# A GeGLU feed-forward kernel on one core: `w_down` staged two rows a step, S3 in one subtraction

## The chip, the cores and the metric

The kernel runs on one core of one Trainium2 chip. The metric is the device time of one execution in microseconds (us); the time of a kernel is the median of its runs. A core has a matmul engine (TensorE, PE in the profile, with its weight loads as PEld), a vector engine (VectorE, DVE), a scalar engine (ScalarE, ACT), a general engine (GpSimd, POOL), and SyncE (SP), which here only issues DMAs. Each engine works through its own queue in order: an instruction that waits holds up all behind it. PSUM, into which TensorE writes, has 8 banks of 128 x 512 fp32.

## The reference

```python
B, S, D, F = 1, 2048, 1024, 3584          # all bf16
# x: (B, S, D); w_gate, w_up: (D, F); w_down: (F, D)
def _gelu(x):
    return jax.nn.gelu(x, approximate=True)

def reference(x, w_gate, w_up, w_down):
    return (_gelu(x @ w_gate) * (x @ w_up)) @ w_down
```

Three matrix products, with Gelu and an elementwise product between them.

## The kernel before, in words

**Seven products for eight.** Each matrix product is made by Winograd's form of Strassen's scheme: both operands are cut into 2 x 2 blocks, sums of blocks are formed (S1 to S4 and a copy of block 22 on the weight side, T1 to T4 and a copy of B22 on the other), and seven block products M1 to M7 take the place of eight. The sums are made in fp32r, so most matmuls read fp32r operands.

**Halves, chunks, pairs.** The 2,048 rows of x are worked in two halves `h` of 1,024 rows, each as two blocks of 512 (`xT[0]`, `xT[1]`, transposed). F has 28 tiles of 128 columns; four tiles make a chunk of `w_gate` and `w_up` (`chunks`, 1 MB each). Two tiles make a *pair*; 14 pairs make a half. The result, `hT`, holds 28 tiles x 1,024 rows in bf16. The free part of `hT` is borrowed before it is written: chunks 0 and 4 lie in its tiles 20 to 27, held M1 results in others.

**The first half runs as** `first_units` (plain products of eight tiles for block 0; the first half of each sum, which is M1, is kept by `hold` and later fetched back into a bank), then `quads` over `MID` (pairs 4, 5), then `quads` over `LEADS` (eight pairs, made of tiles 0 to 7 and 12 to 19, whose M1 is a held one), then the loop over `lead` with two pairs each: lead 10 and lead 12 (pairs 10, 11 and 12, 13), which begin with M1 and M2 of both pairs in plain bf16. Then `down_group` twice: the product with `w_down`.

**A pair in `quads`** issues, for gate (j = 0) and up (j = 1): M5 and M6 (in `LEADS` the order is M5 of gate, M6, M6, M5 of up; elsewhere M6 first), each of 4 matmuls into a bank of 512 columns; ScalarE copies M5 to `m5` and M6 on to the R banks; VectorE adds M5 (`add_m5`, L497); M7 (reads S3); V = R + M5 (L497 again); M3 onto the Q banks (reads S4, needs the addition), M4 onto the R banks. ScalarE applies Gelu to the gate bank, VectorE multiplies with the up bank into `hT` (L305), which frees the bank. Meanwhile the sums of the *next* pair are made: S1, S2, S4 by GpSimd (L449), the copy of A22 by ScalarE (L462), S3 by GpSimd, or by VectorE (L447) where `s3_dve` is set (MID and LEADS).

**The staging.** T2 and T4 of `w_down` are needed four times (two halves, two groups). They are computed once in the first half and kept in DRAM (`t_dram`); the down phase loads them. `stage_load` fetches row block i and row block 14 + i of `w_down` into one `wd_sb` buffer (three of them); `stage_step` is one of three subtractions for row i: t = b12 - b11 (k = 0), t = b22 - t (k = 1, stored as T2), t' = b21 - t (k = 2, stored as T4). 14 rows make 42 steps of 512 columns (L685, stores at L687), with `t` in one of four `o_sb` buffers. The steps are placed by hand, in lists `thens[n][name]` that `quads` runs after a product (`done(n, name)`; "start" is ahead of the pair's first product): each runs on VectorE behind the pair's own work there.

**x of the second half.** Block 1 goes straight into `xT[1]` (DMA transposes at L201). Block 0 has no room yet: `stage_x` transposes it into tiles 24 to 27 of `hT` (L704), and `store_x` writes it to `x_dram` (L709), before pairs 12 and 13 write those tiles.

**Order.** `sp`, `act`, `dve`, `pool` and `pe` chain all instructions of an engine in the order in which the program writes them. Waits for data and for buffers are added by the framework, by regions of memory. All weight rows, t stores, x transposes and x stores go through SP's queue; the chunks of `w_gate` and `w_up` in this stretch go through ScalarE's.

Of the kernel before, what the change touches and what calls it, by code (L numbers as in the profile page):

```python
# [34 lines left out]
def kernel(  # L35
# [50 lines left out]
    o_pool = ctx.enter_context(tc.tile_pool(name="o", bufs=4))  # L86
# [11 lines left out]
    s_late = []  # L98

# [71 lines left out]
    chunks = {}  # L171

    def new_chunk(key):
        if key in ((0, 0), (0, 4)):
            mem, c0 = hT0[:, HF : HF + KD, :].rearrange("p a b -> p (a b)"), 0
        else:
            mem, c0 = w_mem, 2 * CH * (key[1] % 2 if key != (0, 3) else 0)
        chunks[key] = tuple(
            mem[:, c0 + j * CH : c0 + (j + 1) * CH].rearrange(
                "p (a b) -> p a b", b=FG  # L180
            )
            for j in range(2)
        )
# [108 lines left out]
    def gelu(ps, last=False):  # L292

        if last:
            g_sb = o_pool.tile([P, TB], F32, name="o_sb")[:]
        else:
            e0 = 4 * CH + (g_ctr[0] % 4) * 2 * TB
            g_ctr[0] += 1
            g_sb = w_mem[:, e0 : e0 + 2 * TB].bitcast(F32)
        act(nc.scalar.activation(out=g_sb, in_=ps[:], func=ACT.Gelu_apprx_tanh))  # L300
        return g_sb
# [163 lines left out]


    def quads(hT, h, members, nxt, thens, m5_first, plain=True, s3_dve=False):
# [6 lines left out]
        def fetch(n):  # L474
            for j in range(2):
                act(nc.scalar.copy(out=bank2(run[n][4][j]), in_=p_hold(n, j)))
# [32 lines left out]
        if not plain:  # L509
            fetch(0)  # L510
# [9 lines left out]
        for n, (pair, after, then, _, Q_) in enumerate(run):  # L520
# [3 lines left out]
            def prep(j, name, after=after):  # L524
                if after is not None:
                    on_dve = s3_dve and name == "s3"
                    s_sum(after[0], after[1], j, name, on_dve, False)
# [85 lines left out]
    def load_b21(n, q):  # L613
        i0, i1 = q * BPT, min((q + 1) * BPT, NS)
        if i1 < NS:
            w = wd_pool.tile([P, WDT, D], BF16, name="wd_sb")
            w = w[:].rearrange("p a d -> p (a d)")
        else:
            w = o_pool.tile([P, (i1 - i0) * DN], BF16, name="o_sb")[:]
        w = w.rearrange("p (b n) -> p b n", n=DN)  # L620
        src = wdv[:, NS + i0 : NS + i1, 0:DN]
        sp(nc.sync.dma_start(out=w[:, 0 : i1 - i0, :], in_=src))
        b21_tiles[(n, q)] = w
# [41 lines left out]
    NSTEP = 3 * NS  # L665

    def stage_load(i):
        w = wd_pool.tile([P, WDT, D], BF16, name="wd_sb")
        for j in range(2):
            k = j * NS + i  # L670
            sp(nc.sync.dma_start(out=w[:, j : j + 1, :], in_=wdv[:, k : k + 1, :]))
        staged[i] = [w]

    def stage_step(n):
        i, k = n // 3, n % 3
        w = staged[i][0]
        if k != 1:
            staged[i].append(o_pool.tile([P, DN], F32R, name="o_sb")[:])
        t = staged[i][-1]
        in0, in1 = (  # L680
            lambda: (w[:, 0, DN:D], w[:, 0, 0:DN]),
            lambda: (w[:, 1, DN:D], t.bitcast(F32)),
            lambda: (w[:, 1, 0:DN], staged[i][1].bitcast(F32)),
        )[k]()
        dve(nc.vector.tensor_tensor(out=t, in0=in0, in1=in1, op=ALU.subtract))  # L685
        if k > 0:
            sp(nc.sync.dma_start(out=t_dram[:, i, k - 1, :], in_=t.bitcast(F32)))  # L687

# [47 lines left out]
    def down_group(hT, h, grp, then):  # L736
# [65 lines left out]
        def evacuate(bset, l, d, halves=False):  # L802

            outs = []
            for u in range(2):
                if halves and u == 1:
                    r0 = h * SH + t0 + (2 * l + u) * P
                    for bank, c in ((bset[u], 0), (VB[u], DH)):
                        dst = o_pool.tile([P, DN], BF16, name="o_sb")[:, 0:DH]
# [8 lines left out]
                dst = o_pool.tile([P, DN], BF16, name="o_sb")[:]  # L818
# [118 lines left out]
    for h in range(NH):  # L937
# [16 lines left out]
        nstep, loads = len(steps), list(range(3, NS))  # L954
# [9 lines left out]

        def run_loads():
            while loads and 3 * (loads[0] - 2) <= nstep - len(steps):
                stage_load(loads.pop(0))
# [7 lines left out]
        if h == 0:  # L975
            for i in range(3):
                stage_load(i)

            def load_half(c, f0):
                if f0 == 0:  # L980
                    new_chunk((0, c))
                for j in range(2):
# [9 lines left out]
                    "m4": [lambda: new_x(1), lambda: run_steps(1)],  # L992
                },
                {
                    "start": [lambda: run_steps(1)],
                    "m5": [lambda: load_half(3, FA)],
                    "m3": [lambda: run_steps(1), run_loads],
                    "m4": [lambda: run_steps(1)],
# [4 lines left out]
            for n in range(NL):  # L1003
                thens[n]["start"] = [lambda: run_steps(1), run_loads]
                thens[n]["m3"] = [lambda n=n: run_steps(1 + n % 2), run_loads]
# [6 lines left out]
            thens[7]["start"].append(lambda: load_half(5, FA))  # L1012
# [6 lines left out]
        for lead in range(begin, NPAIR, PPG):  # L1019
# [7 lines left out]
            if h == 0:  # L1027
                add(0, "m1", lambda: run_steps(4), run_loads)
                if lead < NPAIR - PPG:
                    add(0, "start", lambda: run_steps(3))  # L1030
                add(1, "start", lambda: run_steps(1))
                for n in range(PPG):
                    add(n, "start", run_loads, run_x)
                    add(n, "m4", store_x, run_loads)
                    add(n, "m3", lambda: run_steps(1), run_loads)
                    add(n, "m4", run_late)
# [122 lines left out]
```

## Time and profile before

| | |
|---|---|
| runs | 544.23, 545.2, 545.32 us; median 545.2 us |
| profiled execution | 543.92 us, span 542.1 us |
| PE, DVE, ACT, POOL busy | 534.5, 385.3, 272.8, 246.3 us |
| steps (L685) | 42, 48.7 us together (28 of 1086 ns, 14 of 1304 ns) |
| S3 on DVE (L447, into s_mem) | 20, some 1.04 us each |
| DMA, `w_down` to `wd_sb`, staging | 28 of 256 KB |
| DMA, `o_sb` to `t_dram` | 28 of 256 KB |

By stage, from the span's start (PE's busy time beside the length): MID ends and LEADS begin near 59 us; LEADS last to 137.7 (DVE busy 76.4 of 78.8 us); lead 10 to 160.5, lead 12 to 187; the down phase of the first half to 275; the second half's pairs to 451 and its down phase to the end.

How to read it: times are of one profiled execution. L481 is the line that issues the matmuls of `quads`, L758 those of the down phase. "idle before, releaser" names what ended an engine's wait. Matmuls are pipelined, so a busy PE is not a PE at its peak: a row of 4 lasts 4 x 0.228 us, though each is shown with about 0.39.

### The profile page before, as it was taken

What the parts mean: (1) busy time and instruction counts of PE and PEld (TensorE: products, weight loads), DVE (VectorE), ACT (ScalarE), POOL (GpSimd) and SP (SyncE); (2) the same over time, 40 slices, a digit from 0 to 9 for tenths busy, and PEclk for the clock granted to TensorE, in tenths of its full rate; (3) what the DMA queues carried; (4) which work ended last, traced back from release to release, by engine and by line L of the source; (5) the groups of instructions that cost most, each with busy time, mean ns of one, the idle gap of its engine ahead of it and who ended that gap; (6) DMA issues with size and microseconds to landing.
All of it is one profiled execution on the core that took longest, in us unless ns stands there. A gap on an engine that the chain in (4) does not pass through costs nothing.

```text
span 542.1 us, 7109 instructions
## 1 busy us (share of the span) xinstructions
PE 534.5 (99%) x2380; PEld 381.1 (70%) x2380; DVE 385.3 (71%) x498; ACT 272.8 (50%) x471; POOL 246.3 (45%) x202
## 2 busy tenths in 40 slices
PE   9999999999999999999999999999999999999997
PEld 4448787777676776767668686767768686866866
DVE  0497999999887999789565253434444659979861
ACT  4465666556554418216565555546555552462270
POOL 0088988988397200000045494949587670000000
PEclk9999999999999999999999999999999999999999
DMA  8963647495767696878960404223140329677846
GB/s 238 273 226 101 211 127 212 117 327 172 243 166 269 203 384 218 301 242 290 321 234 0 157 13 144 73 83 122 34 155 5 151 68 333 230 246 249 290 143 209
DMA packets 98292, 102.70 MB, mean 189 GB/s; under 512 B 18768, under 2 KB 73168, under 8 KB 98256
## 3 DMA queue, kind: packets, MB, share of 16 engines
q1 hardware_dynamic: 71792, 82.53, 47.1%
q10 hardware_dynamic: 26464, 19.73, 12.1%
q8 instruction: 19, 0.31, 0.2%
q14 instruction: 17, 0.14, 0.1%
HBM read 85.98 MB, written 12.58 MB: 182 GB/s over the span
## 4 chain that ended last, share of the span: by engine, by line
PE 90%; DVE 4%; DMA 3%; issue 2%; ACT 1%; SPq 0%; DVEq 0%; ACTq 0%
PE bank L481 53%; PE bank L758 31%; PE bank L342 5%; DVE o_sb L685 2%; DMA t_mem<-t_dram 1%; DMA x_dram<-hT 1%; DVE hT L305 1%; PE bank L232 1%; DVE bank L497 0%; SPq L709 0%; PE bank L324 0%; ACT w_mem L300 0%; ACT bank L542 0%; ACT bank L507 0%; DVE xT L332 0%
## 5 line engine op out<-in xcount | busy, mean ns | idle before, releaser
L481 PE MATMUL bank<-t_mem,s_mem 128*128 128x512 f32 x1096 | 254.7, 392 | 2.9 <-ACT bank L542 0.9
L481 PEld LDWEIGHTS bank<-t_mem,s_mem 128*128 128x128 f32 x1096 | 205.0, 188 | 50.0 <-POOL s_mem L449 2.7
L449 POOL TENSOR_TENSOR s_mem<-w_mem 128x512 fp32r<-128x512 bf16 x80 | 97.1, 1232 | 190.3 <-DVE t_mem L287 99.3
L305 DVE TENSOR_TENSOR hT<-w_mem,bank 128x512 bf16<-128x512 f32 x106 | 71.2, 683 | 69.8 <-PE bank L481 39.5
L497 DVE TENSOR_TENSOR bank<-bank,m 128x512 f32<-128x512 f32 x112 | 72.7, 692 | 42.7 <-ACT m L537 41.0
L758 PE MATMUL bank<-t_mem,s_mem 128*128 128x512 f32 x416 | 98.4, 394 | 0.4 <-DMA t_mem<-t_dram 0.4
L300 ACT ACTIVATE w_mem<-bank 128x512 f32<-128x512 f32 x106 | 62.6, 596 | 60.7 <-DVE bank L497 39.0
L758 PEld LDWEIGHTS bank<-t_mem,s_mem 128*128 128x128 f32 x416 | 78.0, 188 | 17.8 <-DVE t_mem L660 0.8
L481 PE MATMUL bank<-xT,w_mem 128*128 128x512 bf16 x320 | 71.0, 379 | 0.4 <-DVE hT L305 0.4
L660 DVE TENSOR_TENSOR t_mem<-w_mem 128x1024 fp32r<-128x1024 bf16 x56 | 65.7, 1218 | 0.4 <-PE bank L481 0.4
L449 POOL TENSOR_TENSOR s_mem<-w_mem,s_mem 128x512 fp32r<-128x512 bf16 x46 | 61.2, 1352 | 3.4 <-PE bank L481 3.4
L481 PEld LDWEIGHTS <-w_mem 128*128 128x128 bf16 x320 | 30.6, 98 | 38.5 <-issue 3.0
L449 POOL TENSOR_TENSOR s_mem<-s_mem,w_mem 128x512 fp32r<-128x512 f32 x46 | 57.3, 1265 | 0.2
L542 ACT COPY bank<-bank 128x512 f32<-128x512 f32 x56 | 31.9, 571 | 29.6 <-PE bank L481 20.4
L462 ACT CAST s_mem<-w_mem 128x512 fp32r<-128x512 bf16 x48 | 29.5, 616 | 24.4 <-PE bank L481 23.2
L537 ACT COPY m<-bank 128x512 f32<-128x512 f32 x56 | 32.7, 588 | 17.5 <-PE bank L481 15.8
L758 PEld LDWEIGHTS <-hT 128*128 128x128 bf16 x224 | 21.2, 98 | 26.7 <-issue 2.1
L823 ACT CAST o_sb<-bank 128x512 bf16<-128x512 f32 x27 | 14.8, 586 | 33.8 <-PE bank L758 31.2
L685 DVE TENSOR_TENSOR o_sb<-wd_sb,o_sb 128x512 fp32r<-128x512 bf16 x28 | 30.4, 1086 | 0.3
L758 PE MATMUL bank<-t_mem,s_late 128*128 128x512 f32 (+1 forms) x132 | 30.3, 382 | 0.0
L507 ACT COPY bank<-bank 128x512 f32<-128x512 f32 x40 | 22.8, 570 | 12.6 <-PE bank L481 12.6
L730 DVE TENSOR_TENSOR s_mem<-hT 128x512 fp32r<-128x512 bf16 x36 | 23.5, 686 | 7.0 <-PE bank L758 7.0
(61 smaller groups left out, 398.6 us busy)
## 6 DMA issues: line engine op xcount, KB each, us to landing
t_mem<-t_dram SPq DMA_DIRECT2D x56, 512.0 KB, 5.5
wd_sb<-in_w_down_dram SPq DMA_DIRECT2D x28, 256.0 KB, 3.5
t_dram<-o_sb SPq DMA_DIRECT2D x28, 256.0 KB, 2.4
w_mem<-in_w_gate_dram ACTq DMA_DIRECT2D x6, 1024.0 KB, 5.3
w_mem<-in_w_up_dram ACTq DMA_DIRECT2D x6, 1024.0 KB, 8.1
wd_sb<-in_w_down_dram SPq DMA_DIRECT2D x12, 512.0 KB, 7.6
w_mem<-in_w_gate_dram SPq DMA_DIRECT2D x8, 512.0 KB, 5.5
w_mem<-in_w_up_dram SPq DMA_DIRECT2D x8, 512.0 KB, 7.2
```

What stands on the lines that cost most here:

```text
L300: act(nc.scalar.activation(out=g_sb, in_=ps[:], func=ACT.Gelu_apprx_tanh))
L305: nc.vector.tensor_tensor(out=hT[:, fc, tb * TB : (tb + 1) * TB], in0=g_sb, in1=ps[:], op=ALU.mult,)
L342: nc.tensor.matmul(banks[held[u][j]][:], lhsT=w_sb[:, kd, f0 : f0 + P], rhs=xT[0][:, kd, :], start=kd == 0, stop=kd in (KH - 1, KD - 1), s ...
L449: pool(nc.gpsimd.tensor_tensor(out=t, in0=in0, in1=in1, op=op))
L462: act(nc.scalar.copy(out=t, in_=a(1, 1)))
L481: nc.tensor.matmul(banks[bank][:], lhsT=lhs[:, c, :], rhs=rhs[:, c, :], start=start and c == 0, stop=c == KH - 1, skip_group_check=True,)
L497: nc.vector.tensor_tensor(out=banks[dst][:], in0=banks[src][:], in1=m5[:], op=ALU.add)
L537: act(nc.scalar.copy(out=m5[j][:], in_=banks[V_[j]][:]))
L542: act(nc.scalar.copy(out=banks[R_[j]][:], in_=banks[Q_[j]][:]))
L660: dve(nc.vector.tensor_tensor(out=t, in0=in0, in1=in1, op=ALU.subtract))
L685: dve(nc.vector.tensor_tensor(out=t, in0=in0, in1=in1, op=ALU.subtract))
L758: nc.tensor.matmul(banks[bank][:, c0:c1], lhsT=lhs(i, u), rhs=rhs(i)[:, c0:c1], start=start and i == 0, stop=stop and i == NS - 1, skip_gr ...
```

## The change

One `o_sb` buffer pool of four is replaced by one strip of memory (`o_mem`) of four slots, handed out in turn by `new_o`; a slot is 128 x 512 fp32. A step now works on two rows at once: 1,024 columns, two slots, so that the strip holds two such tiles, one for k = 0 and 1, the other for k = 2. `stage_load` brings two row blocks in one DMA of 512 KB; a load m is issued when `first_step(m)` steps have been issued. There are 21 steps, one for each pair of MID and LEADS (at "m3") and eleven in leads 10 and 12: two at "m1" and two at "start" of each, one after M3 of pairs 10, 11 and 12. `s3_both` makes both S3 of a pair in one subtraction, after M7 of up. The M1 of the first LEADS pair is fetched after M7 of the second MID pair, not at the head of LEADS. `stage_x` of block 0 and `store_x` move from leads 10 and 12 into the last LEADS pair (start, m3, m4).

```diff
--- before.py
+++ after.py
@@ -83,7 +83,6 @@
     hT_pool = ctx.enter_context(tc.tile_pool(name="hT", bufs=1))
     wd_pool = ctx.enter_context(tc.tile_pool(name="wd", bufs=3))
     m_pool = ctx.enter_context(tc.tile_pool(name="m5", bufs=1))
-    o_pool = ctx.enter_context(tc.tile_pool(name="o", bufs=4))
     dram_pool = ctx.enter_context(
         tc.tile_pool(name="dram", bufs=1, space=bass.MemoryType.DRAM)
     )
@@ -96,6 +95,17 @@
 
     s_mem = shared_pool.tile([P, 2 * 5 * KH * P], F32R, name="s_mem")
     s_late = []
+
+    NO = 4
+    o_mem = shared_pool.tile([P, NO * 2 * DN], BF16, name="o_sb")
+    o_ctr = [0]
+
+    def new_o(dtype, n=1):
+        o0 = o_ctr[0] % NO * DN
+        assert o0 + n * DN <= NO * DN
+        o_ctr[0] += n
+        o = o_mem[:, 2 * o0 : 2 * (o0 + n * DN)]
+        return o if dtype == BF16 else o.bitcast(dtype)
 
     CH = KD * FG
     w_mem = shared_pool.tile([P, 4 * CH + (NS - 4) * DN], BF16, name="w_mem")
@@ -168,13 +178,16 @@
         return banks[bank][:].rearrange("p (b c) -> p b c", b=2)
 
     xs0 = w_mem[:, 4 * CH : 4 * CH + TSB * D].rearrange("p (a b) -> p a b", b=D)
-    chunks = {}
+    chunks, both = {}, {}
 
     def new_chunk(key):
         if key in ((0, 0), (0, 4)):
             mem, c0 = hT0[:, HF : HF + KD, :].rearrange("p a b -> p (a b)"), 0
         else:
             mem, c0 = w_mem, 2 * CH * (key[1] % 2 if key != (0, 3) else 0)
+        both[key] = mem[:, c0 : c0 + 2 * CH].rearrange(
+            "p (j a b) -> p j a b", j=2, b=FG
+        )
         chunks[key] = tuple(
             mem[:, c0 + j * CH : c0 + (j + 1) * CH].rearrange(
                 "p (a b) -> p a b", b=FG
@@ -292,7 +305,7 @@
     def gelu(ps, last=False):
 
         if last:
-            g_sb = o_pool.tile([P, TB], F32, name="o_sb")[:]
+            g_sb = new_o(F32)
         else:
             e0 = 4 * CH + (g_ctr[0] % 4) * 2 * TB
             g_ctr[0] += 1
@@ -463,6 +476,24 @@
 
     S_NAMES = ("s1", "s2", "s3", "s4", "a22")
 
+    def s3_both(h, pair):
+        s0 = 2 * S_NAMES.index("s3") * KH * P
+        t = s_mem[:, s0 : s0 + 2 * KH * P]
+        t = t.rearrange("p (j a b) -> p j a b", j=2, b=P)
+        for j in range(2):
+            ssum[(h, pair, j, "s3")] = t[:, j]
+        ins = []
+        for tile_ in tiles_of(h, pair):
+            f0 = tile_ % FPG * P
+            ins.append(both[(h, tile_ // FPG)][:, :, half(0), f0 : f0 + P])
+        dve(
+            nc.vector.tensor_tensor(out=t, in0=ins[0], in1=ins[1], op=ALU.subtract)
+        )
+
+
+    def fetch_to(bset, n):
+        for j in range(2):
+            act(nc.scalar.copy(out=bank2(bset[j]), in_=p_hold(n, j)))
 
     def quads(hT, h, members, nxt, thens, m5_first, plain=True, s3_dve=False):
 
@@ -472,8 +503,7 @@
             run.append((pair, after, thens[n], (PB, RB)[n % 2], (QB, VB)[n % 2]))
 
         def fetch(n):
-            for j in range(2):
-                act(nc.scalar.copy(out=bank2(run[n][4][j]), in_=p_hold(n, j)))
+            fetch_to(run[n][4], n)
 
         def mm(bank, lhs, rhs, start):
             for c in range(KH):
@@ -506,8 +536,6 @@
                 mm(first_[j], block((h, "p", pair), j, 0, 0), b11, True)
                 act(nc.scalar.copy(out=banks[q_[j]][:], in_=banks[first_[j]][:]))
         done(0, "m1")
-        if not plain:
-            fetch(0)
         for pair, _, _, first_, _ in run if plain else ():
             for j in range(2):
                 mm(first_[j], block((h, "p", pair), j, 0, 1), b21, False)
@@ -523,8 +551,10 @@
 
             def prep(j, name, after=after):
                 if after is not None:
-                    on_dve = s3_dve and name == "s3"
-                    s_sum(after[0], after[1], j, name, on_dve, False)
+                    if not s3_dve or name != "s3":
+                        s_sum(after[0], after[1], j, name)
+                    elif j == 1:
+                        s3_both(*after)
 
             def s(j, name, pair=pair):
                 return ssum[(h, pair, j, name)]
@@ -616,7 +646,7 @@
             w = wd_pool.tile([P, WDT, D], BF16, name="wd_sb")
             w = w[:].rearrange("p a d -> p (a d)")
         else:
-            w = o_pool.tile([P, (i1 - i0) * DN], BF16, name="o_sb")[:]
+            w = new_o(BF16)[:, 0 : (i1 - i0) * DN]
         w = w.rearrange("p (b n) -> p b n", n=DN)
         src = wdv[:, NS + i0 : NS + i1, 0:DN]
         sp(nc.sync.dma_start(out=w[:, 0 : i1 - i0, :], in_=src))
@@ -662,30 +692,33 @@
 
 
     staged = {}
-    NSTEP = 3 * NS
-
-    def stage_load(i):
+    NSTEP = 3 * NS // 2
+
+    def stage_load(m):
+        i = 2 * (m // 2)
         w = wd_pool.tile([P, WDT, D], BF16, name="wd_sb")
-        for j in range(2):
-            k = j * NS + i
-            sp(nc.sync.dma_start(out=w[:, j : j + 1, :], in_=wdv[:, k : k + 1, :]))
-        staged[i] = [w]
+        k = m % 2 * NS + i
+        sp(nc.sync.dma_start(out=w[:], in_=wdv[:, k : k + 2, :]))
+        staged[(i, m % 2)] = w
 
     def stage_step(n):
-        i, k = n // 3, n % 3
-        w = staged[i][0]
+        i, k = 2 * (n // 3), n % 3
+        w = staged[(i, min(k, 1))]
         if k != 1:
-            staged[i].append(o_pool.tile([P, DN], F32R, name="o_sb")[:])
-        t = staged[i][-1]
+            if o_ctr[0] % 2:
+                o_ctr[0] += 1
+            t = new_o(F32R, 2).rearrange("p (a b) -> p a b", b=DN)
+            staged[(i, "t")], t_last = t, staged.get((i, "t"))
+        t = staged[(i, "t")]
         in0, in1 = (
-            lambda: (w[:, 0, DN:D], w[:, 0, 0:DN]),
-            lambda: (w[:, 1, DN:D], t.bitcast(F32)),
-            lambda: (w[:, 1, 0:DN], staged[i][1].bitcast(F32)),
+            lambda: (w[:, :, DN:D], w[:, :, 0:DN]),
+            lambda: (w[:, :, DN:D], t.bitcast(F32)),
+            lambda: (w[:, :, 0:DN], t_last.bitcast(F32)),
         )[k]()
         dve(nc.vector.tensor_tensor(out=t, in0=in0, in1=in1, op=ALU.subtract))
         if k > 0:
-            sp(nc.sync.dma_start(out=t_dram[:, i, k - 1, :], in_=t.bitcast(F32)))
-
+            dst = t_dram[:, i : i + 2, k - 1, :]
+            sp(nc.sync.dma_start(out=dst, in_=t.bitcast(F32)))
 
 
     staged_x = []
@@ -806,7 +839,7 @@
                 if halves and u == 1:
                     r0 = h * SH + t0 + (2 * l + u) * P
                     for bank, c in ((bset[u], 0), (VB[u], DH)):
-                        dst = o_pool.tile([P, DN], BF16, name="o_sb")[:, 0:DH]
+                        dst = new_o(BF16)[:, 0:DH]
                         src = banks[bank][:, c : c + DH]
                         if c == 0:
                             dve(nc.vector.tensor_copy(out=dst, in_=src))
@@ -815,7 +848,7 @@
                         c0 = d * DN + c
                         outs.append((out2[r0 : r0 + P, c0 : c0 + DH], dst))
                     continue
-                dst = o_pool.tile([P, DN], BF16, name="o_sb")[:]
+                dst = new_o(BF16)[:, 0:DN]
                 r0 = h * SH + t0 + (2 * l + u) * P
                 if last_grp and u == 0:
                     dve(nc.vector.tensor_copy(out=dst, in_=banks[bset[u]][:]))
@@ -951,7 +984,7 @@
         s3_late = range(6, NS, 2)
         steps = [lambda k=k: stage_step(k) for k in range(NSTEP)]
         lates = [lambda i=i: s_down(hT, 0, "s3", i, i + 2) for i in s3_late]
-        nstep, loads = len(steps), list(range(3, NS))
+        nstep, loads = len(steps), list(range(NS))
 
         def run_steps(n):
             for f in steps[:n]:
@@ -962,8 +995,12 @@
             if lates:
                 lates.pop(0)()
 
+        def first_step(m):
+            u = m // 2
+            return max(0, 3 * u - (2 if m % 2 else 3)) if m > 2 else 0
+
         def run_loads():
-            while loads and 3 * (loads[0] - 2) <= nstep - len(steps):
+            while loads and first_step(loads[0]) <= nstep - len(steps):
                 stage_load(loads.pop(0))
 
         def run_x():
@@ -973,8 +1010,7 @@
             del xs[:m]
 
         if h == 0:
-            for i in range(3):
-                stage_load(i)
+            run_loads()
 
             def load_half(c, f0):
                 if f0 == 0:
@@ -989,27 +1025,28 @@
                     ],
                     "m5": [lambda: load_half(3, 0)],
                     "m3": [lambda: run_steps(1)],
-                    "m4": [lambda: new_x(1), lambda: run_steps(1)],
+                    "m4": [lambda: new_x(1), run_loads],
                 },
                 {
-                    "start": [lambda: run_steps(1)],
                     "m5": [lambda: load_half(3, FA)],
+                    "m7": [lambda: fetch_to(QB, 0)],
                     "m3": [lambda: run_steps(1), run_loads],
-                    "m4": [lambda: run_steps(1)],
                 },
             ]
             quads(hT, h, MID, (h, LEADS[0]), thens, False, True, True)
             thens = [{} for _ in LEADS]
             for n in range(NL):
-                thens[n]["start"] = [lambda: run_steps(1), run_loads]
-                thens[n]["m3"] = [lambda n=n: run_steps(1 + n % 2), run_loads]
+                thens[n]["start"] = []
+                thens[n]["m3"] = [lambda: run_steps(1), run_loads]
             for n in range(NL // 2):
                 thens[2 + n]["start"].append(run_x)
             thens[1]["start"].append(lambda: load_half(4, 0))
             thens[3]["start"].append(lambda: load_half(4, FA))
             thens[5]["start"].append(lambda: load_half(5, 0))
             thens[5]["m7"] = [lambda: load_chunk((0, 6))]
-            thens[7]["start"].append(lambda: load_half(5, FA))
+            thens[7]["start"] += [lambda: load_half(5, FA), run_x]
+            thens[7]["m3"].append(run_x)
+            thens[7]["m4"] = [store_x]
             quads(hT, h, LEADS, (h, begin), thens, True, False, True)
             s_late.append(
                 shared_pool.tile([P, NL // 2 * TB], F32R, name="s_late")
@@ -1025,13 +1062,10 @@
 
             add(1, "m3", lambda key=(h, lead // PPG + 2): load_chunk(key))
             if h == 0:
-                add(0, "m1", lambda: run_steps(4), run_loads)
-                if lead < NPAIR - PPG:
-                    add(0, "start", lambda: run_steps(3))
-                add(1, "start", lambda: run_steps(1))
-                for n in range(PPG):
-                    add(n, "start", run_loads, run_x)
-                    add(n, "m4", store_x, run_loads)
+                add(0, "m1", lambda: run_steps(2), run_loads)
+                few = lead == NPAIR - PPG
+                add(0, "start", lambda: run_steps(2), run_loads)
+                for n in range(1 if few else PPG):
                     add(n, "m3", lambda: run_steps(1), run_loads)
                     add(n, "m4", run_late)
             for n, pair in enumerate(members):
```

## The prediction

> **What bounds the kernel now.** First the page's head and chain, to see which engine sets the end.
>
> ```profile
> span 542.1 us, 7109 instructions
> PE 534.5 (99%) x2380; PEld 381.1 (70%) x2380; DVE 385.3 (71%) x498; ACT 272.8 (50%) x471; POOL 246.3 (45%) x202
> PE 90%; DVE 4%; DMA 3%; issue 2%; ACT 1%; SPq 0%; DVEq 0%; ACTq 0%
> ```
>
> TensorE is the bound, and the change does not touch its instructions. So it can win only PE's stalls, and lose by making new ones. Next the table of waits, PE's rows:
>
> ```profile
> PE bank L481 <- ACT bank L542: 0.9, 1, 0.9
> PE bank L481 <- DVE bank L497: 0.9, 3, 0.3
> PE bank L481 <- ACT bank L476: 0.5, 1, 0.5
> PE bank L481 <- DVE hT L305: 0.4, 1, 0.4
> PE bank L758 <- DMA t_mem<-t_dram: 0.4, 1, 0.4
> ```
>
> A stalled matmul also loses its overlap with the one before, so I take a stall's price from the ends of neighbouring matmul records: 0.228 us apart as a rule (0.216 with bf16), and more at a stall. The excess, by place: 0.35 at 55.0; 0.72 at 60.3; 0.40 + 0.56 at 82.4 and 83.9, 0.40 + 0.55 at 101.6 and 103.1, 0.41 + 0.53 at 120.7 and 122.2; 0.57 at 138.1; 1.19 + 0.33 at 173.2 and 174.5; 0.63 at 205.1. Sum 6.6 us: all that can be won. The chain in order of time says who caused two of them:
>
> ```profile
> 78.97 1.65 DVE o_sb L685
> 80.62 0.60 DVE hT L305
> 81.22 1.47 DVE o_sb L685
> 82.69 0.62 DVE bank L497
> ...
> 163.72 7.53 DMA x_dram<-hT
> 171.26 0.02 issue
> 171.28 0.70 DVE hT L305
> ```
>
> At 80 us the staging steps (L685) stand in VectorE's queue in front of the product (L305) that frees a bank, and of the addition (L497) that PE needs. At 171 us a product waits until `hT` has been written out to `x_dram`. Last, VectorE and SP by time, around the steps and around lead 10:
>
> ```profile
> 77.45 1.60 DVE L685 TENSOR_TENSOR o_sb<-wd_sb,o_sb 128x512 fp32r<-128x512 bf16 x1
> 78.97 1.65 DVE L685 TENSOR_TENSOR o_sb<-wd_sb 128x512 fp32r<-128x512 bf16 x1
> 142.88 0.69 DVE L685 TENSOR_TENSOR o_sb<-wd_sb,o_sb 128x512 fp32r<-128x512 bf16 x1
> ...
> 146.32 5.05 SPq L704 DMA_TRANSPOSE hT<-in_x_dram  x4
> 151.46 0.53 SPq L687 DMA_DIRECT2D t_dram<-o_sb  x1
> ...
> 153.07 1.92 SPq L709 DMA_DIRECT2D x_dram<-hT  x4
> ```
>
> A step of 512 columns takes 0.69 us while GpSimd rests and 1.6 while it works; on SP four transposes cost 5.05 us of issue, four x stores 1.92.
>
> **The change, part by part.** *Steps.* 42 steps cost 28 x 1.086 + 14 x 1.304 = 48.7 us. A 1,024-column subtraction costs 1.22 alone (L660, 1218 ns) and 2.13 beside GpSimd (L287 with an fp32 operand, 2133 ns): 21 cost 26 to 45 us. In the 512-column rows a step waits for the running GpSimd instruction (1.16 us) and then runs, so I take 1.07 plus a wait of 0 to 1.16.
>
> *Both S3.* 20 subtractions of about 1.05 become 10 at 1.22 to 2.13, 0 to 9 us of VectorE. The first half moves behind the second addition; its reader is the next pair's M7, 9 us later, which covers it.
>
> *LEADS.* Eight pairs; PE needs 40 x 0.228 = 9.1 us for one. VectorE after the second M5 copy: 3 additions at 0.6, S3, 2 products at 0.6, the step, 1 product: 0.7 + 1.8 + 1.2 + 0.6 + two large ones. With 2.13 each that is 8.6 of the 9.05 us allowed before the bank is missed. So the 2.85 us at 82 to 122 go. What is late next there is POOL: 6 x 1.16 of its own plus at most 2 x 1.07 blocked is 9.1, just PE's pace; its S4 has 3 us in hand.
>
> *Fetch.* Two ScalarE copies (0.59 each) move from the head of LEADS into the second MID pair, where ScalarE has 0.87 us idle at 57 us. They pass only Gelu of Q, whose product queues behind VectorE anyway: nothing lost, 0.72 won. MID loses its steps at m4 and start: 0.35 at most, 0.2 taken, since the one step left is larger.
>
> *Loads.* 28 issues of 256 KB become 14 of 512 KB, 0.46 us of SP each (0.92 for two). They land in 3.5 to 7.6 us and are called two to four steps (9 us each in LEADS) ahead: covered. Only SP's place counts, below.
>
> *x staged earlier.* Eight transposes and eight stores leave lead 10 for the last LEADS pair. The product at 171 us then finds `hT` stored: 1.52 won. The last w_down step goes out of pair 13 and its store out of the queue before the t2 loads: the loads land back to back there (1.35 us apart), and with 256 KB less in front and an earlier start the 0.63 goes. The stall at 138.1 stays within 0.1: one large step ends at 136.96 where two small ones ended at 137.04.
> Won: 0.2 + 0.72 + 2.85 + 1.52 + 0.63 + 0.1 = 6.0 us (5.0 to 6.6).
>
> *What it costs.* The strip has two halves now: the first subtraction of each row pair writes half A, which the second rewrites and stores. The first of the next pair must wait until that store has landed; one step a pair gives it 18 us. But in lead 10 two steps run at m1 (numbers 10, 11) and two at start (12, 13), and step 10's store stands in SP's queue behind what was moved there. In the old run's times: step 9 (LEADS 7, m3) starts behind GpSimd's instruction of 134.73 to 135.89 and ends at 136.96. SP's next load needs its buffer: 137.0 to 137.5. Four transposes, 5.05: 142.6. Eight x stores, 2 x 1.92: 146.6. Only then step 10's store, ready since about 140. It lands 2.0 us after issue when 256 KB (median 2.4), 0.65 more for twice that: 149.3. Step 12 would have run at 143; it waits, and behind it in VectorE's queue step 13 and the M5 additions. 149.3 + 2 x 1.2 + 0.69 = 152.4. PE ends its 24 matmuls M6, M5, M7 at 147.65, and M3 needs the addition: a new stall of 4.8 us. Nothing covers it: ScalarE's Gelu and GpSimd's S4 wait for the same additions and matmuls. Ends: 3.2 if step 9 meets no GpSimd and the store lands in 2.0; 9.5 if it lands as late as the store of 88.79 (5.5 us) and both steps take 2.13. I stay near the low end, since SP's chain has rows of its own and no chunk load is in flight then. At lead 12 the same pair of steps (16, then 18) lies 5 us apart with SP free: its store lands first, no stall.
>
> **Sum.** 542.1 - 6.0 + 4.8 = 540.9 us of span; the profiled run took 543.92 for 542.1, so 542.7. It lies 1.3 under the median of the runs, 545.2 (544.23 to 545.32); I put the difference, -1.2, on the median: 544.0 us.
>
> **Rivals.** *B: the clock falls in the new stall.* The first seven matmuls took 3.04 us, 0.43 each; the trace's clock record is full from 3.6 us on, 2.8 us after the first of them, and goes to half at 542.9, 3.9 us after the last matmul's end. The longest stall so far, 1.2 us, left it alone. A stall of 4.8 is longer than 3.9, but one fall is one sample. After it, 2.8 us at half rate cost 1.4: 545.4 (up to 547 if it takes twice that). The Trainium skill, "TensorE: Matmul & The Clock Gate", Part 1, has the clock fall after one idle window of about 3.4 us that runs free of the kernel; the trace's two changes are in keeping with that. By that page a stall of 4.8 us holds a whole window in about 4 runs of 10 (an estimate), and the sum would be the 544.0 in the others.
>
> *C: no real stall at lead 10*, if the transposes get in earlier or the store finds SP free. Then the 6.0 us stand less 0 to 2: 539.2 to 541.2, say 540.2. For it: nothing was late there before. Against: one SP queue in written order, and rows for each of its pieces.
>
> *D: VectorE and GpSimd block each other in LEADS; the other side.* If S3 and the step of a pair take more than 9.05 - 4.3 = 4.75 us together, VectorE sets the pace and the 2.85 us stay: 544.0 + 2.85 = 546.9, and 8 us more for each us beyond. Against: twice 2.13 is 4.3. The Trainium skill, "SBUF — State Buffer", Who interferes with whom, says that of a VectorE instruction with two SBUF inputs and a GpSimd one that reads SBUF the later blocks for the whole of the other; the 512-column rows agree (1599 against 677 ns). By that rule alone a large one costs at most 1.07 + 1.16, and D would not come.
>
> *E: the store lands 2.3 us or more later than I have it*: 546.3 to 550.
>
> **Numbers.** A, the forecast, 0.33; B 0.27; C 0.17; D 0.13; E 0.10. A alone spans 542.5 to 545.8 (stall 3.2 to 6.6). Within 0.2% of 545.2 is 544.1 to 546.3, about what this kernel's measurement can tell. A lies on that border: 0.18 faster, 0.14 same, 0.01 slower; B 0.03, 0.16, 0.08; C all faster; D and E slower. Faster 0.38, same 0.30, slower 0.32. For 8 in 10 the range needs most of C and D: 540.3 to 548.0.
>
> **What would show it.** Right: PE's row "bank L481 <- DVE bank L497" with one wait of 4 to 5 us around 144 us; VectorE idle some 6 us before an L685, released by DMA t_dram<-o_sb; SP in one unbroken row L704, L709, L687; no chain through L685 at 80, 100 and 119 us, none through x_dram at 165; L685 at 1.2 to 2.2. Wrong: no such idle time (C), half clock behind it (B), stalls that stay in every second LEADS pair (D).

## The result, and the profile after

The changed kernel takes 549.2 us (four runs, 547.95 to 549.57) against 545.22: slower, a ratio of 1.0073 (95% interval 1.0053 to 1.0094). That lies above the range of 540.3 to 548.0 and 5.2 us above the 544.0 forecast. Its profiled execution took 549.52 us, 5.6 more than that of before (543.92).

The page of the changed kernel: span, engines, the granted clock by slices, and the chain's shares.

```profile
span 547.7 us, 7014 instructions
PE 535.0 (98%) x2380; PEld 383.8 (70%) x2380; DVE 379.9 (69%) x467; ACT 274.0 (50%) x471; POOL 254.9 (47%) x202
PEclk9999999999979999999999999999999999999999
PE 95%; DVE 2%; issue 1%; SPq 1%; DMA 1%; ACT 0%; DVEq 0%
```

PE's busy time is what it was; one slice of 40 has a lower clock. The chain's share on VectorE has halved, and yet the span is longer. PE's rows in the table of waits say where:

```profile
PE bank L511 <- DVE bank L527: 7.3, 2, 6.9
PE bank L511 <- DVE hT L318: 0.9, 2, 0.5
```

Five kinds of short wait have become two, and one of them is a single wait of 6.9 us (L527 is the old L497, L318 the old L305, L718 the old L685). The same chain of work in order of time, at lead 10 of the changed kernel:

```profile
139.44 0.40 SPq L737
...
143.76 0.41 SPq L742
144.17 0.06 issue
144.23 0.02 SPq L721
144.25 0.04 issue
144.28 2.81 DMA t_dram<-o_sb
147.09 0.03 issue
147.12 0.05 DVEq L718
147.17 0.04 issue
147.22 1.77 DVE o_sb L718
148.98 0.02 issue
149.01 2.06 DVE o_sb L718
151.06 0.62 DVE bank L527
```

Here is the predicted loss, link by link: the end of the x transposes (L737), the x stores (L742), the store of step 10 (L721) and its landing, steps 12 and 13, the addition that PE waits for. VectorE by time (first fence) shows the wait itself, and that steps 10 and 11 were done by 137.9; SP by time (second fence) shows what stood ahead of their stores:

```profile
135.42 2.47 DVE L718 TENSOR_TENSOR o_sb<-wd_sb,o_sb 128x1024 fp32r<-128x1024 bf16 x2
139.53 0.69 DVE L318 TENSOR_TENSOR hT<-w_mem,bank 128x512 bf16<-128x512 f32 x1 [1.01 <-PE bank L511]
147.22 1.76 DVE L718 TENSOR_TENSOR o_sb<-wd_sb 128x1024 fp32r<-128x1024 bf16 x1 [7.00 <-DMA t_dram<-o_sb]
149.01 2.06 DVE L718 TENSOR_TENSOR o_sb<-wd_sb,o_sb 128x1024 fp32r<-128x1024 bf16 x1
```

```profile
134.80 5.04 SPq L737 DMA_TRANSPOSE hT<-in_x_dram  x4
139.89 4.28 SPq L742 DMA_DIRECT2D x_dram<-hT  x8
144.28 0.93 SPq L721 DMA_DIRECT2D t_dram<-o_sb  x2
```

Last, stretches of the changed kernel (us, busy time of PE, PEld, DVE, ACT, POOL with instructions, then the clock, the DMA share, GB/s):

```profile
146.00:149.30 3.30, 0.00 (x0) 0.00 (x0) 2.05 (x2) 0.00 (x0) 3.30 (x3) 1.00 0.96 314
149.40:156.10 6.70, 4.28 (x10) 3.45 (x11) 5.18 (x7) 1.19 (x2) 2.13 (x3) 0.50 0.57 186
156.20:160.00 3.80, 3.80 (x18) 3.17 (x17) 3.06 (x4) 2.62 (x5) 0.69 (x1) 1.00 0.30 107
```

After the stall PE runs at half clock until 156.2 us: eight matmuls end 0.427 us apart and a ninth 0.37, where 0.228 is the rule, 1.7 us in all.

A count of all of PE's excess, from the ends of neighbouring matmuls in both profiles, closes the account:

| place | before | after |
|---|---|---|
| 33 to 58 us | 0.35 | 0.62 |
| LEADS | 3.58 | 0 |
| end of LEADS | 0.57 | 0.58 |
| lead 10, stall / half clock | 0 | 7.4 / 1.7 |
| lead 12 | 1.52 | 0.75 |
| down phase | 0.63 | 0 |

6.6 us before, 11.1 after: 4.5 more. The first matmul of `quads` ends 0.73 us later (33.90 against 33.17), and the span ends 0.6 later after the last matmul. The 0.62 at 37 us stood at 0 to 0.26 in the other kernels with this code, and the start moved between 33.2 and 34.6 from profile to profile: neither belongs to the change. Without the 0.62 the excess differs by 3.9 us, near the 4.0 between the medians. (The table lists 0.35 at 55 us before, and the 37 us stall after, in one row.)

### The profile page after: what moved, and what is told of

It is laid out like the page before. It is cut to its first block, busy times and chain, and to the rows that moved or that the text cites. A ratio compares the mean times of both kernels' runs of the same rounds, so it can differ in the third digit from the quotient of the medians.

```text
span 547.7 us, 7014 instructions
## 1 busy us (share of the span) xinstructions
PE 535.0 (98%) x2380; PEld 383.8 (70%) x2380; DVE 379.9 (69%) x467; ACT 274.0 (50%) x471; POOL 254.9 (47%) x202
## 4 chain that ended last, share of the span: by engine, by line
PE 95%; DVE 2%; issue 1%; SPq 1%; DMA 1%; ACT 0%; DVEq 0%
PE bank L511 57%; PE bank L791 32%; PE bank L355 5%; DVE o_sb L718 1%; DVE hT L318 1%; SPq L742 1%; PE bank L245 1%; DMA t_dram<-o_sb 1%; PE bank L337 0%; DVE bank L527 0%; SPq L737 0%; ACT o_sb L847 0%; DVEq L718 0%; DVE wd_sb L763 0%; DVEq L318 0%
## 5 line engine op out<-in xcount | busy, mean ns | idle before, releaser
L462 POOL TENSOR_TENSOR s_mem<-w_mem 128x512 fp32r<-128x512 bf16 x80 | 101.0, 1281 | 186.0 <-DVE t_mem L300 94.8
L318 DVE TENSOR_TENSOR hT<-w_mem,bank 128x512 bf16<-128x512 f32 x106 | 71.1, 684 | 68.9 <-PE bank L511 40.3
L527 DVE TENSOR_TENSOR bank<-bank,m 128x512 f32<-128x512 f32 x112 | 72.3, 693 | 47.3 <-ACT m L567 45.1
L462 POOL TENSOR_TENSOR s_mem<-w_mem,s_mem 128x512 fp32r<-128x512 bf16 x46 | 65.1, 1434 | 7.9 <-PE bank L511 7.9
L462 POOL TENSOR_TENSOR s_mem<-s_mem,w_mem 128x512 fp32r<-128x512 f32 x46 | 54.7, 1208 | 0.2
L791 PEld LDWEIGHTS bank<-t_mem,s_late 128*128 128x128 f32 x132 | 24.4, 188 | 4.9
```

Of the source, the lines that this page charges most:

```text
L318: nc.vector.tensor_tensor(out=hT[:, fc, tb * TB : (tb + 1) * TB], in0=g_sb, in1=ps[:], op=ALU.mult,)
L462: pool(nc.gpsimd.tensor_tensor(out=t, in0=in0, in1=in1, op=op))
L527: nc.vector.tensor_tensor(out=banks[dst][:], in0=banks[src][:], in1=m5[:], op=ALU.add)
L791: nc.tensor.matmul(banks[bank][:, c0:c1], lhsT=lhs(i, u), rhs=rhs(i)[:, c0:c1], start=start and i == 0, stop=stop and i == NS - 1, skip_gr ...
```

## The experiments

Each edit is to the changed kernel, unless it says otherwise; `...` marks lines left out, and `few` is true in lead 12 alone. The kernel before was measured anew beside each group of experiments (545.0 to 545.1 us); a difference from the changed kernel rests on its four runs (547.95 to 549.57) and is good to about 1 us. Further down, a number in brackets is that of an experiment.

**1. The second half of the x work behind the step stores.**

```diff
-            thens[7]["m3"].append(run_x)
-            thens[7]["m4"] = [store_x]
...
+                if not few:
+                    add(0, "m1", run_x)
+                    add(0, "m4", store_x)
```

> The changed kernel with one move: the second four x transposes go behind steps 10 and 11 of lead 10 (at m1), and the x stores to M4 of pair 10. Nothing else changes: two halves of the strip, steps of 1,024 columns, same places of the steps. Theory (the store of step 10 lands late because SP's queue holds the moved x work in front of it): the store is issued some 8 us earlier, step 12 no longer waits, the stall of 7.4 us at 152 us and the nine matmuls at half clock (1.8 us) go; about 540 us against 549.2. Rival 1 (two subtractions of 1,024 columns in a row are themselves too long for lead 10, beside GpSimd): the stall falls by less than half; 545 us or more. Rival 2 (the strip's two halves are too few wherever two steps follow each other): a wait of VectorE for the store remains, some 3 us; 543 us or more.

Measured: 542.82 us, 0.9964 of before (0.9953 to 0.9975). At lead 10 the stall is gone whole: step 12 starts at 139.40 us, right behind the product, and steps 12 and 13 take 1.22 and 1.23. So neither the two halves nor the steps' length make the 7.4 us; the place of the store in SP's queue does. It is 2.8 us short of the 540 expected, since lead 12, now earlier, has a stall of its own. VectorE by time in this kernel:

```profile
167.33 1.53 DVE L718 TENSOR_TENSOR o_sb<-wd_sb 128x1024 fp32r<-128x1024 bf16 x1 [0.37 <-DMA t_dram<-o_sb]
168.90 2.06 DVE L718 TENSOR_TENSOR o_sb<-wd_sb,o_sb 128x1024 fp32r<-128x1024 bf16 x1
170.89 2.48 DVE L527 TENSOR_TENSOR bank<-bank,m 128x512 f32<-128x512 f32 x4
```

Two large steps beside GpSimd stand in front of the additions; PE stands 2.5 us and then loses 1.6 at half clock. Step 16's store, issued at 161.51, landed 5.8 us later; two loads of 1 MB of `w_down` rows issued before it landed at 162.1 and 164.7. Here SP was free, and the delay lies between issue and landing; 0.37 us of it is left as VectorE's wait.

**2. Only the x stores moved, the transposes left.**

```diff
-            thens[7]["m4"] = [store_x]
...
+                if not few:
+                    add(0, "m4", store_x)
```

> The changed kernel, with only the eight x stores moved from M4 of the last LEADS pair to M4 of pair 10; the transposes stay in front of step 10's store. Theory: the store of step 10 is issued 4.3 us earlier, near 140 us, and lands near 142.7; VectorE waits some 2.5 us in place of 7; the stall of PE is 2 to 3 us and too short for the clock to fall (3.9 us was seen to pass before it fell): 542.5 us, 6.5 less than the changed kernel. If the clock falls all the same: 544. Rival 1 (length of the steps): no change by this move, 549.

Measured: 544.9 us, 0.9999 of before (0.9986 to 1.0013). VectorE's wait for the store shrank from 7.0 to 2.8 us and PE's stall from 7.4 to 2.7, as expected; and the clock fell all the same, for 1.6 us of loss: the time is 0.9 above the 544 given for that case. (By the granted clock it fell in nine of the ten runs; in one, of 543.8 us, it stayed at 1.0.) My bound from the record of before (a fall 3.9 us after the last matmul) was wrong: here it fell 3.7 us after the last one, when PE had been at work again for 1.2.

**3. The x stores twice.**

```diff
-    def store_x():
+    def store_x(clear=True):
...
-        staged_x.clear()
+        if clear:
+            staged_x.clear()
...
-            thens[7]["m4"] = [store_x]
+            thens[7]["m4"] = [lambda: store_x(False), store_x]
```

> The changed kernel with the eight x stores issued twice at the same place (the same bytes to the same place). Theory: 4.3 us more of SP's queue ahead of step 10's store, so it lands 4.3 us later and PE's stall grows from 7.4 to 11.7 us: 553.5 us; the time at half clock stays that of the clock's rise, about 1.8 us (0 to 1.7 more or less by where the clock's interval lies). Rival 1 (length of the steps): no change, 549.

Measured: 551.61 us, 1.0115 of before (1.01 to 1.0129). VectorE's wait for the store grew from 7.0 to 11.0 us, by the 4 us of SP time added. PE's stall grew less, from 7.4 to 10.0 and not to 11.7, because GpSimd had finished by then and steps 12 and 13 took 1.23 and 1.22 in place of 1.76 and 2.06. So the dose acts on the wait one for one, and shows a second term: GpSimd's work beside the two steps.

**4. The stall kept, PE kept busy.**

```diff
+                if not few:
+                    add(0, "m5", lambda: [warm(PB[0]) for _ in range(26)])
```

The added matmuls compute nothing that is used.

> The changed kernel with 26 matmuls of constants added between M5 and M7 of pair 10, into a bank that is free there: PE works 5.6 us of what was idle, and M7 follows. VectorE's and SP's work is the same, so M3 still waits for the same addition. Theory (the clock's fall is a cost of its own, beside the wait): PE's idle time before M3 is under 2 us, the clock stays full, and the nine matmuls at 0.427 us take 0.228: 1.8 us less than the changed kernel, 547.4. Rival (the half clock lies beside work that waits for VectorE anyway): no change, 549.2.

Measured: 545.93 us, 1.0014 of before (1.0005 to 1.0022); 3.3 us under the changed kernel, not 1.8. VectorE's wait for the store is as long as before:

```profile
147.27 1.22 DVE L718 TENSOR_TENSOR o_sb<-wd_sb 128x1024 fp32r<-128x1024 bf16 x1 [7.09 <-DMA t_dram<-o_sb]
148.53 1.23 DVE L718 TENSOR_TENSOR o_sb<-wd_sb,o_sb 128x1024 fp32r<-128x1024 bf16 x1
```

The clock record stays full to the end, so the fall is a cost of its own: 1.7 us, by the nine matmuls that no longer run slow. Another 1.4 us was not expected: M7 comes later here, and with it GpSimd's two S3 subtractions, which wait for M7; so the steps run alone. The experiment moves two things; experiment 5 takes the second by itself.

**5. S3 in lead 10 made by VectorE.**

```diff
-            quads(hT, h, members, nxt, thens, lead == 0)
+            s3_dve = h == 0 and lead == begin
+            quads(hT, h, members, nxt, thens, lead == 0, True, s3_dve)
```

> The changed kernel with both S3 of pairs 11 and 12 made by VectorE in lead 10, in place of two GpSimd subtractions each. It takes GpSimd's last two instructions (146.8 to 150.0 us in the changed kernel) from beside steps 12 and 13. Theory (1.4 us of the stall is the two steps at 1.76 and 2.06 us beside GpSimd's S3 where I reckoned 1.2): both steps take 1.22, PE's stall falls from 7.4 to 6.0 us: 547.8. Rival (the steps are long for another reason): no change, 549.2, or more for the subtractions that VectorE has taken over.

Measured: 546.4 us, 1.0033 of before (1.002 to 1.0045). The wait for the store is unchanged (7.1 us), the stall is 6.2 us, 1.2 less. In the profile the half clock lasts 3.4 us in place of 6.8 and costs 1.0 in place of 1.7, and lead 12's 0.7 is gone: with these the median is 2.8 less, where I had 1.4. (By the granted clock the shorter half clock came in three of the eight runs.) GpSimd in the changed kernel, at the place:

```profile
144.53 2.26 POOL L462 TENSOR_TENSOR s_mem<-s_mem,w_mem 128x512 fp32r<-128x512 f32 x2
146.75 3.23 POOL L462 TENSOR_TENSOR s_mem<-w_mem 128x512 fp32r<-128x512 bf16 x2
```

The second row is S3 of pair 11; it lies beside steps 12 and 13 (147.22 to 151.06).

**6. The x move alone, on the kernel before.**

```diff
+            thens[7]["m4"] = [store_x]
...
-            thens[7]["start"].append(lambda: load_half(5, FA))
+            thens[7]["start"] += [lambda: load_half(5, FA), run_x]
+            thens[7]["m3"].append(run_x)
...
-                    add(n, "start", run_loads, run_x)
-                    add(n, "m4", store_x, run_loads)
+                    add(n, "start", run_loads)
+                    add(n, "m4", run_loads)
```

> The kernel before, with one part of the change: x of block 0 staged in the last LEADS pair (four transposes at start, four after M3, eight stores after M4). Steps of 512 columns, four buffers, S3 and fetch as before. Theory (the x work in SP's queue ahead of the step stores is what costs, whatever the step's size): the first step of the row that takes the buffer of a row stored at m1 waits as in the changed kernel; VectorE waits 5 to 7 us for a t store, PE loses 5 us or more at lead 10 and 1.8 at half clock, and the 1.5 us at 173 are won: 549 to 551. Rival (only the strip with two halves makes the wait; four buffers suffice): no stall, 543.5.

Measured: 551.27 us, 1.0112 of before (1.0097 to 1.0126). Its table of waits has the line

```profile
DVE o_sb L685 <- DMA t_dram<-o_sb: 5.6, 1, 5.6
```

and PE a stall of 5.3 us and a half clock at lead 10, with steps of one row and four buffers. So I had named the strip's two halves as the condition, and they are not needed: one part of the change, the place of the x work, carries the loss, whatever the size of a step.

**7. The x move undone, all else changed.**

```diff
-            thens[7]["start"] += [lambda: load_half(5, FA), run_x]
-            thens[7]["m3"].append(run_x)
-            thens[7]["m4"] = [store_x]
+            thens[7]["start"] += [lambda: load_half(5, FA)]
...
+                if not few:
+                    for n in range(PPG):
+                        add(n, "start", run_x)
+                        add(n, "m4", store_x)
```

> The changed kernel with x staged as before, in pairs 10 and 11 (four transposes at each start, four stores after each M4); all else as changed. Theory: the store of step 10 finds SP free, no wait of VectorE for it at lead 10 beyond 1 to 3 us (landing 2.8 us after an issue near 136.7, step 12 due near 139.5), no fall of the clock there; the 60, 82 to 122 us stalls stay won (3.6 us), the late x store at 171 us may stay or grow: 541 to 544. Rival (length of the steps): 547 or more.

Measured: 547.45 us, 1.0045 of before (1.0031 to 1.0058): a miss, and a time that the rival had. Lead 10 is clean, as expected, and LEADS too, so the length of the steps costs nothing there. But lead 12 loses 8.9 us, with two stalls and a clock at half for 10.2 us.

```profile
DVE hT L318 <- DMA x_dram<-hT: 3.5, 1, 3.5
...
PE bank L511 <- ACT bank L572: 2.8, 1, 2.8
PE bank L511 <- DVE bank L527: 1.9, 1, 1.9
```

The product's wait for `x_dram` was 2.0 us before and is 3.5 now: the product is due 2.4 us earlier, while the x stores land only 0.9 us earlier, 8.5 to 9.3 us after their issue and behind two loads of 1 MB of `w_down` rows issued at 159.25 and 159.88. The second stall is that of the steps: step 18 waits 1.5 us for a t store, then 18 and 19 stand in front of the addition. So at its old place the x work costs more here than it did before. Whether the place itself or the loads in front of it are at fault was not tested; the changed kernel's error is to put the x work ahead of the store of step 10 ([1], [6]).

**8. A version beyond: experiment 1 with lead 12 spread.** To experiment 1 it adds

```diff
-                add(0, "start", lambda: run_steps(2), run_loads)
-                for n in range(1 if few else PPG):
+                add(0, "start", lambda k=1 if few else 2: run_steps(k), run_loads)
+                for n in range(PPG):
...
-                if pair == NPAIR - 2 - (h == 0):
+                if pair == NPAIR - 2:
...
-                        "start" if h else "m7",
+                        "start",
```

> The version with the x stores behind (542.8 us; there PE still stood 2.5 us at 172 us and lost 1.8 at half clock, VectorE's steps 18 and 19 standing in front of the addition, step 18 waiting for a store that landed 5.8 us after issue behind 2 MB of w_down rows), and in it two more moves: in lead 12 one step at start and one after M3 of each pair, and the two loads of w_down rows 0 to 7 at the start of pair 12 in place of after M7 of pair 11. If those two are the cause: no stall over 0.6 us between 40 and 190 us, full clock throughout, 538.5 us. If the large steps are too long for lead 12 in themselves: 541 or more.

Measured: 541.41 us, 0.9931 of before (0.9917 to 0.9944). Lines of its page, and PE's rows in the waits:

```profile
span 539.3 us, 7013 instructions
PEclk9999999999999999999999999999999999999999
```

```profile
PE bank L511 <- DVE hT L318: 0.4, 1, 0.4
PE bank L511 <- DVE bank L527: 0.2, 1, 0.2
```

No stall over 0.6 us from 40 to 190 us, and full clock: as expected. The time is 2.9 us above the 538.5 that I had and in the rival's range, though no stall of the rival's kind is there. The two moves were not taken apart; with the loads issued behind it, at 164.44, step 16's store landed 2.75 us after its issue, where [1] had 5.8. In the profile PE's excess is 2.0 us, 4.7 less than in the kernel before; against that stand a start 0.9 us later and 0.9 more from the last matmul to the end.

**9. The fetch alone, on the kernel before.**

```diff
...
-        if not plain:
-            fetch(0)
...
+                    "m7": [lambda: fetch_to(QB, 0)],
```

> The kernel before, with the fetch of the first held M1 moved to after M7 of the second MID pair, nothing else. Theory: the stall at 60.3 us (0.72 us) goes and nothing takes its place: 544.3 against 545.0. Rival: the two copies delay Gelu of Q and a bank comes free later; the stall only moves: 545.0.

Measured: 545.63 us, 1.0011 of before (1.0002 to 1.002). What the rival forecast came, but not on its path: the stall at 60.3 us goes and one of 1.04 us stands at 66.3. The products are not delayed (additions and products both lie 1.2 us later than before); PE waits for VectorE, whose two steps after M4 and at the next pair's start took 2.63 us together where they took 1.77:

```profile
PE bank L484 <- DVE bank L500: 1.8, 4, 0.8
```

Four such waits, where the kernel before has three.

**10. Both S3 in one, alone, on the kernel before.** `s3_both` and its two lines in `prep`, nothing else.

> The kernel before, with both S3 of a pair in one subtraction, nothing else. Theory: the stalls at 82, 101 and 120 us (2.85 us) come from two steps after M3 of every second pair, so they shrink by what one wait for GpSimd costs (0.3 to 0.5 us each) and do not all go: 543 to 544.5. Rival (S3 in two is itself the cause): the 2.85 us go, 542.1.

Measured: 544.93 us, 0.9996 of before (0.9986 to 1.0007): no difference. The three double stalls of LEADS stay, at 0.48 + 0.48 us each where they were 0.40 + 0.55. So neither forecast came: the stalls did not shrink, and S3 in two is not their cause. That leaves the steps in front of them.

**11. The version of experiment 8 with S3 in two again.** `prep` as in the kernel before.

> The version of 541.4 us (x stores behind, lead 12 spread, w_down rows later) with S3 made in two subtractions of 512 columns, as before the change. Theory (one large step a pair leaves VectorE half a us in hand, S3 in two costs 0.1 to 1.1 us more a pair): between no change and 1 us in LEADS, 541.4 to 542.5. Rival (S3 in one is what won LEADS): the three stalls come back, 544 or more.

Measured: 540.63 us, 0.9916 of before (0.99 to 0.9931), and no stall in LEADS. It overlaps with experiment 8's interval: the joined S3 wins nothing that these runs can tell. It is the fastest version measured here.

## Why the prediction was wrong

**The mechanism was right, its size and one side effect were not.** What was forecast as the cost is the cost: VectorE stands behind step 10's store (7.0 us, [1] and [6]), SP is one unbroken row, and no chain runs through the steps or `x_dram` at the old places. (That the strip's two halves are a condition for it was wrong: [6] has the wait with four buffers.) What failed are three terms of the loss.

**First, the last term of the stall**, "149.3 + 2 x 1.2 + 0.69". Everything up to the landing fits: the four transposes took 5.04 us (5.05), the eight stores 4.28 (3.84), the landing 2.81 (2.65). But steps 12 and 13 took 1.76 and 2.06, not 1.2 each. I had the price of a step beside GpSimd, up to 2.13, and used it for the range's far end only; for the sum I took the price alone, arguing from SP's queue and never asking what GpSimd does at that moment. It makes S3 of pair 11 there, since S3 goes to VectorE only in MID and LEADS. That is 1.4 us ([3], [4], [5]). The trace of the kernel before had the row, at the very time (149.3) at which I let step 12 start:

```profile
149.53 2.74 POOL L449 TENSOR_TENSOR s_mem<-w_mem 128x512 fp32r<-128x512 bf16 x2
```

With 0.4 more for the stores on SP, and 0.8 in the landing, the hand-overs and the end of M7, 4.8 became 7.4.

**Second, the clock was a rival where it belonged in the sum.** I gave it 0.27 with a price of 1.4; it fell in all runs of the changed kernel that were recorded (mean granted clock 0.994 in each of four) and cost 1.7 ([4]). In [1] it fell in a stall of 2.3 us. Forecast plus these two, 544.0 + 2.6 + 1.7, is 548.3; with the next point it is 549.0.

**Third, "no stall" at lead 12** was off by 0.7 us: the store did land in time, but steps 18 and 19 took 1.22 and 2.08 us in front of the addition.

**The gains** came as forecast: LEADS 3.6 (0.72 + 2.85), 1.5 at 173 us, 0.6 at 205, and what had been 0.35 at 55 us: 6.1 against 6.0. But the parts do not add up one by one. The fetch, for which I had 0.72, wins nothing by itself ([9]), so that this term came out only with the others, and S3 in one wins nothing at all ([10], [11]). What is left to free LEADS is one large step a pair in place of two or three small ones; that was not run alone. The steps' group shows that they were not cheap for it:

```profile
L718 DVE TENSOR_TENSOR o_sb<-wd_sb,o_sb 128x1024 fp32r<-128x1024 bf16 x14 | 27.1, 1932 | 0.1
L718 DVE TENSOR_TENSOR o_sb<-wd_sb 128x1024 fp32r<-128x1024 bf16 x7 | 13.1, 1870 | 7.0 <-DMA t_dram<-o_sb 7.0
L490 DVE TENSOR_TENSOR s_mem<-w_mem,hT 128x1024 fp32r<-128x1024 bf16 x4 | 8.5, 2124 | 0.0
```

The steps (the first two rows; the third is S3 in one) took 40.2 us together against 48.7, inside the 26 to 45 given: near the upper end, because 18 of the 21 took 1.6 us or more beside GpSimd's work, where one alone takes 1.22.

**The rivals.** C did not come: one queue in written order does what its rows say. D did not come: S3 and step took about 2.1 us each, as bounded, and LEADS has no stall. E did not come as such: the landing was within 0.2 us. The direction was wrong because two numbers of like size and opposite sign (6.0 and 4.8) were set against each other by their centres, with a gain of 1.2 us left; the gains came out as given, and all that was missed (2.6, 1.7 and 0.7 us) lay on the side of the loss.

## What to carry to other kernels

When DMA issues are moved to an earlier place in a queue, list what else is issued from that queue behind them, and follow each until somebody waits for its landing; here eight stores and four transposes, 9.3 us of issue, cost more than the stall that they cured. Price each instruction of a new chain by what runs beside it at that time, not by its row alone. And count a stall of over 2 us on TensorE with the half-rate stretch behind it: here stalls of 2.3 us and more brought one in most runs, at 1.0 to 1.8 us each.

## What the runs showed of the hardware

**The clock falls without a whole interval of idleness.** Between the first matmuls and the last, the stretches at half rate in these profiles' clock records last 3.41, 6.83 or 10.24 us, one to three times 3.41, and in each profile all changes of the clock lie on one grid of that step (in the kernel before, 3.58 and 542.88 us, 158 steps apart). In experiment 1 PE stood still for only 2.3 us, and fell:

```profile
169.40:172.60 3.20, 0.93 (x5) 0.79 (x5) 3.20 (x4) 0.00 (x0) 3.20 (x3) 1.00 0.23 86
172.70:176.00 3.30, 3.30 (x9) 2.63 (x8) 2.63 (x5) 1.09 (x2) 3.30 (x4) 0.50 0.17 63
```

By the profile's busy time, in the 3.41 us ahead of the fall PE was busy for 1.14 us here, for 1.19 in experiment 2, for 1.41 in experiment 6 and 1.35 in 7. In the kernel before the stall of 1.2 us at 173 left it alone: of the interval on this grid that holds it (170.83 to 174.24) PE was busy for 2.38 us. In experiment 5 even 1.76 us kept the full clock for one more interval; the fall came after the next, in which PE stood still:

```profile
142.45:145.86 3.41, 1.76 (x8) 1.13 (x6) 0.00 (x0) 0.57 (x1) 3.41 (x4) 1.00 0.79 279
145.86:149.27 3.41, 0.00 (x0) 0.00 (x0) 2.59 (x3) 0.00 (x0) 0.22 (x1) 1.00 0.99 311
```

The Trainium skill, "TensorE: Matmul & The Clock Gate", Part 1, gives an interval of 3413 ns that runs free of the kernel, and these lengths agree with it; that it takes a whole idle one to fall does not hold here: one that was busy for 41% was enough. In these runs the share that keeps the clock lies between that and the 52% of experiment 5. To come back it took more: in experiment 7 an interval busy for 2.05 us (60%) left the clock at half, in experiment 5 one busy for 2.81 us (82%) ended it.

**A larger VectorE subtraction holds GpSimd longer.** A GpSimd subtraction of 512 columns takes 1.16 us by itself, about 1.62 beside a VectorE subtraction of 512 columns, and 2.15 beside one of 1,024: 0.5 and 1.0 us more, where those subtractions take 0.68 and 1.22 alone. GpSimd's busy time rose from 246.3 to 254.9 us; in LEADS PE waited for none of it.
